# The second bank of a paired product gets a tile of its own: three matrix stages on one Trainium2 core

## The chip, the cores and the metric

The kernel is one program on one core of a Trainium2 chip. TensorE (PE) multiplies, VectorE (DVE), ScalarE (ACT) and GpSimd (POOL) do the elementwise work, SyncE (SP) issues the transfers. The metric is the device time of one execution in microseconds (us), lower is better.

## The reference

Attention over 4 batches, 8 heads, 576 positions and 64 columns a head, half of the heads with a local mask and half with a strided one, followed by two feed-forward layers over the 2304 tokens that it gives:

```
attn = softmax(where(mask, q @ k.T / 8, -1e9));  x = attn @ v          # to 2304 x 512
h = x @ w_in;  x = maximum(0.01 * h, h) @ w_out                        # 512 -> 2048 -> 512
h = x @ w_in2; out = (maximum(h, 0) + log1p(exp(-abs(h)))) @ w_out2    # 512 -> 2048 -> 512
```

## The kernel before

Every product is made of three 16-bit products: each operand is cut into a high and a low part, and high x high, high x low and low x high are added up in PSUM. The tokens go through the layers in units of 288 (first layer) and 256 (second layer). Units 0 to 3 (batches 0 and 1) take the first layer's first product one by one. Units 4 and 5 (batch 2), and units 6 and 7 (batch 3), take it in pairs, by a scheme of seven products of half-size blocks in place of eight (`plan_first_pair`). That scheme, run twice, is what this document is about; "the first pair stage" is units 4 and 5, "the second pair stage" units 6 and 7.

A pair stage has eight blocks, numbered k = 0 to 7 here. One block is seven groups of six matmuls on PE (`group`, L1236, each matmul 128 x 128 by 128 x 288) into three PSUM accumulators, and between them short steps on ACT and DVE that read an accumulator. Their names in the code:

- accumulator a takes p1, then p2 on top of it. Between the two, `t1` (ACT, L1257) copies it to the SBUF tile n1; after p2, `bend11` (ACT, L1272, in the rows `t<-h,gs`) reads it for the last time.
- accumulator b takes p6, p7 and p4 on top of each other. After p6, `u2` (DVE, L1260) adds it to n1 and writes n2; after p7, `u3` (DVE, L1260) does the same for n2's other half; after p4, `c21` (DVE, L1260) reads it for the last time.
- accumulator c takes p5 and then p3, and is read by `c22` and `c12` (DVE, L1260, in the rows `t<-c,t`).
- then come `bend21`, `bend2` (ACT, L1272), the cut into high parts (ACT, L1279) and low parts (POOL, L1283).

So p2 needs t1, u2 needs p6 and t1, p7 needs u2, u3 needs p7, p4 and c22 need u3, p3 needs c22. In the rows of PE, `h<-x,w` is p1 or p2, `h<-sums` is p6 or p7, `h<-sums,w` is p4, `c<-sums` is p5 and `c<-x,w` is p3.

PSUM has four pools: `ps_mm` ("mm", two tiles of two banks), `ps_sc` ("sc", the scores: one tile of two banks), `ps_pt` ("pt", one bank) and `ps_pv` ("po", the value products: one bank). In the kernel before, a and b of a block are the two banks of one "mm" tile, `st["ab"]`; c is the "pt" bank.

The order of everything is written out: `Plan` collects 2018 steps with their needs and the PSUM places that they take and free, and runs them in the order of the table `ORDER`. Each engine takes its instructions in that order. The waits between engines are put in from the tiles that each instruction reads and writes. Beside the pair stages the same table places the last steps of batch 3's attention, the preparation of the second layer's weights (long DVE and ACT steps over 2048 columns, L267, L322, L333, L1497, L1515, L1519) and the products into the first layer's output (`plan_second`, names M and S in the table's steps; `o<-g,pair` in the rows of PE, moved out by ACT, L1330).

Of the kernel before, what the change touches and what calls it, by code (L numbers as in the profile page):

```python
# [11 lines left out]
F32 = mybir.dt.float32  # L12
# [8 lines left out]
P = 128  # L21
# [137 lines left out]
def build(tc, qt, kl, ks, v, wi1, wo1, wi2, wo2, mloc, mstr, msml, out):  # L159
    nc = tc.nc  # L160
    with ExitStack() as ctx:
# [1051 lines left out]
        def plan_first_pair(u, after, places, rank):  # L1213
            b = u // 2
            out, begun = [None] * NF, []
            for k in range(NP):
# [27 lines left out]
                def p1(st=st, q=q, i=i, start=start):  # L1244
                    start()
                    group(st, 0, raw(q, 0, i), xs_of(0, 0), True)
# [643 lines left out]
```

## Time and profile before

| | us |
|---|---|
| median of 3 runs | 833.27 (832.67 to 833.44) |
| the profiled execution | 833.24 |
| its span, first to last instruction | 831.4 |
| PE busy | 806.7 |
| DVE busy | 603.2 |
| ACT busy | 537.3 |

The profiled execution's own time is 1.84 us longer than its span, and 0.03 us from the median. A matmul's busy time here runs until its modelled end, so that the next one starts while it is still "busy"; idle time of PE is time in which no matmul was in flight.

### The profile page before, as it was taken

To read this page: it belongs to the slowest core of one execution; us is meant where nothing else is said; L and a number is where in the kernel's file an instruction comes from. 1 tells how busy PE (TensorE), PEld (TensorE's weight loads), DVE (VectorE), ACT (ScalarE), POOL (GpSimd) and SP (SyncE) were. 2 spreads that over 40 slices of the span, in tenths; PEclk is the share of its full clock that TensorE was granted. 3 is DMA by queue.
4 is the path that set the end of the run, shared out by engine and by line. 5 is a ranking of instruction groups with operands and counts; after the bars stand their busy time and mean duration, and the time that the engine had idled before them with its cause. 6 is when DMAs were issued, how large, how long until landed. Compare 5 with 4: busy or idle time off the path is not lost.

```text
span 831.4 us, 18276 instructions
## 1 busy us (share of the span) xinstructions
PE 806.7 (97%) x7531; PEld 667.6 (80%) x7531; DVE 603.2 (73%) x1367; ACT 537.3 (65%) x957; POOL 253.1 (30%) x193
## 2 busy tenths in 40 slices
PE   9999999999999998998899999999999999999997
PEld 6677777777777766776677888888888888888886
DVE  4999987668899857997678478776656656745654
ACT  2798877764444666355554298776778668766773
POOL 1236946460131243003420024322232222322231
PEclk9999999999999999999999999999999999999999
DMA  9926705342522220631322500100110010000010
GB/s 341 419 103 234 247 16 109 62 135 93 147 62 41 62 102 2 218 130 41 122 81 91 194 4 1 52 1 2 50 53 2 2 52 1 27 1 2 1 52 26
DMA packets 39699, 70.23 MB, mean 84 GB/s; under 512 B 21088, under 2 KB 31168, under 8 KB 37056
## 3 DMA queue, kind: packets, MB, share of 16 engines
q1 hardware_dynamic: 39328, 68.84, 25.1%
q8 instruction: 59, 0.97, 0.5%
q10 hardware_dynamic: 288, 0.23, 0.1%
q14 instruction: 24, 0.20, 0.1%
HBM read 54.84 MB, written 9.44 MB: 77 GB/s over the span
## 4 chain that ended last, share of the span: by engine, by line
PE 82%; DVE 11%; ACT 3%; issue 2%; DMA 2%; DVEq 0%; POOL 0%; ACTq 0%; POOLq 0%
PE o L765 13%; PE o L767 13%; PE o L766 13%; PE h L765 10%; PE h L767 10%; PE h L766 10%; PE h L1236 6%; PE c L1236 2%; PE idle L197 1%; PE ps L490 1%; DVE t L1260 1%; DMA pair<-wi_dram 1%; PE po L700 1%; DVE pair L333 1%; PE ps L495 1%
## 5 line engine op out<-in xcount | busy, mean ns | idle before, releaser
L765 PE MATMUL h<-x,w 128*128 128x256 f16 (+1 forms) x832 | 230.4, 277 | 0.6 <-ACT t L786 0.6
L767 PE MATMUL h<-x,w 128*128 128x256 f16 (+1 forms) x832 | 230.2, 277 | 0.0
L766 PE MATMUL h<-x,w 128*128 128x256 f16 (+1 forms) x832 | 230.2, 277 | 0.0
L1659 POOL TENSOR_TENSOR rs<-rs,t 128x512 f32<-128x512 f32 x72 | 98.2, 1365 | 281.7 <-ACT t L1655 145.9
L765 PE MATMUL o<-g,pair 128*128 128x288 f16 x512 | 146.5, 286 | 0.0
L767 PE MATMUL o<-g,pair 128*128 128x288 f16 x512 | 146.4, 286 | 0.0
L766 PE MATMUL o<-g,pair 128*128 128x288 f16 x512 | 146.4, 286 | 0.0
L1667 DVE TENSOR_TENSOR rs<-rs 128x128 f32<-128x128 f32 x288 | 76.9, 309 | 75.1 <-POOL rs L1659 72.4
L1675 DVE SCALAR_TENSOR_TENSOR gr<-rs,x2g,gr 128x896 f16<-128x896 f32 x72 | 84.9, 1184 | 40.5 <-ACT gr L1671 39.6
L1671 ACT ACTIVATE gr<-rs,x2g 128x896 f16<-128x896 f32 x72 | 74.3, 1036 | 36.6 <-DVE rs L1667 36.6
L765 PEld LDWEIGHTS <-w 128*128 128x128 f16 x832 | 81.4, 98 | 13.9 <-issue 0.2
L766 PEld LDWEIGHTS <-w 128*128 128x128 f16 x832 | 81.4, 98 | 13.0 <-issue 0.7
L767 PEld LDWEIGHTS <-w 128*128 128x128 f16 x832 | 81.4, 98 | 12.9
L614 POOL TENSOR_TENSOR s<-s,sm 128x288 f32<-128x288 f32 (+6 forms) x48 | 43.0, 913 | 147.8 <-DVE sm L609 84.1
L1283 POOL TENSOR_TENSOR g<-t,g 128x576 f16<-128x576 f32 x32 | 45.1, 1415 | 113.0 <-ACT g L1279 111.4
L1642 ACT ACTIVATE t<-h,x2s 128x512 f32<-128x512 f32 x72 | 48.9, 680 | 35.1 <-PE h L767 35.0
L792 POOL TENSOR_TENSOR g<-t,g 128x576 f16<-128x576 f32 x32 | 54.4, 1720 | 22.0 <-ACT g L789 21.8
L765 PEld LDWEIGHTS <-pair 128*128 128x128 f16 x512 | 50.1, 98 | 13.5
L767 PEld LDWEIGHTS <-pair 128*128 128x128 f16 x512 | 50.1, 98 | 12.6
L766 PEld LDWEIGHTS <-pair 128*128 128x128 f16 x512 | 50.1, 98 | 12.3
L765 PE MATMUL o<-w,gr 128*128 128x256 f16 x216 | 58.9, 273 | 0.0
L766 PE MATMUL o<-w,gr 128*128 128x256 f16 x216 | 58.9, 273 | 0.0
(162 smaller groups left out, 1742.6 us busy)
## 6 DMA issues: line engine op xcount, KB each, us to landing
pair<-wi_dram SPq DMA_DIRECT2D x8, 2048.0 KB, 9.7
pair<-wo_dram SPq DMA_DIRECT2D x8, 2048.0 KB, 8.0
x<-t SPq DMA_DIRECT2D x16, 288.0 KB, 2.6
x<-x SPq DMA_DIRECT2D x9, 512.0 KB, 5.1
out_dram<-pair SPq DMA_DIRECT2D x18, 256.0 KB, 2.6
v<-v_dram SPq DMA_DIRECT2D x2, 1856.0 KB, 13.6
pair<-v_dram SPq DMA_DIRECT2D x2, 1408.0 KB, 6.8
q<-qt_dram SPq DMA_DIRECT2D x6, 288.0 KB, 5.9
```

Of the source, the lines that this page charges most:

```text
L614: nc.gpsimd.tensor_tensor(out=sv, in0=sv, in1=rs, op=ALU.mult)
L765: nc.tensor.matmul(ps, ah, bh, start=first, stop=False)
L766: nc.tensor.matmul(ps, ah, bl, start=False, stop=False)
L767: nc.tensor.matmul(ps, al, bh, start=False, stop=last)
L792: nc.gpsimd.tensor_tensor(out=g[:, 1, f : f + 2, :], in0=t, in1=g[:, 0, f : f + 2, :], op=ALU.subtract)
L1236: nc.tensor.matmul(ps, w[:, c], x[:, c], start=first and c == n == 0, stop=c == 1 and n == 2, skip_group_check=not first)
L1283: nc.gpsimd.tensor_tensor(out=g_[:, 1, fs, :], in0=st[f"n{j + 1}"], in1=g_[:, 0, fs, :], op=ALU.subtract)
L1642: nc.scalar.activation(t, self.ps[k], AF.Prelu, scale=self.sc[:, k // 2 : k // 2 + 1], alpha=-1.0)
L1659: nc.gpsimd.tensor_tensor(out=r, in0=r, in1=self.a[k], op=ALU.add)
L1667: nc.vector.tensor_tensor(out=r[:, o], in0=r[:, x], in1=r[:, y], op=op)
L1671: nc.scalar.activation(self.a[k][:, 0], self.r[k][:, 1:], AF.Copy, scale=self.ag[:, k // 2 : k // 2 + 1])
L1675: nc.vector.scalar_tensor_tensor(out=a[:, 1], in0=self.r[k][:, 1:], scalar=self.ag[:, k // 2 : k // 2 + 1], in1=a[:, 0], op0=ALU.mult, op1 ...
```

## The change

Accumulator b leaves the tile that it shared with a. Accumulator a is now the first bank of a two-bank "mm" tile of its own (the second bank of it stays unused), and b is a tile named `b`: the "sc" pool's in blocks 0, 2, 4 and 6, the "po" pool's in blocks 1, 3, 5 and 7. The place of a is given back after `bend11` and no longer after `bend21`; that of b after `c21`. The products of unit 6 into the first layer's output, which took the "sc" tile, now take an "mm" tile as those of the other units do. One condition is changed for the matmuls that fill PE's waits before the first products (`idle`). The table `ORDER` is made anew, all of it.

```diff
 ORDER = (
-    0, 1, 9, 10, 11, 8, 12, 2, 13, 14, 15, 16, 25, 41, 26, 17, 4, 27, 3, 42, 18, 5, 19, 20, 21, 22, 28, 29, 30, 31,
+    0, 9, 10, 11, 12, 1, 13, 25, 26, 8, 114, 14, 2, 41, 27, 3, 15, 19, 16, 17, 28, 4, 42, 43, 18, 29, 20, 21, 5, 30,
...
-                        if n > 0 and y not in o.take and free[y][i] is not None and free[y][i] <= clock[o.eng]:
+                        if n > 0 and y not in o.take and None not in free[y] and free[y][i] <= clock[o.eng]:
...
-                    st["ab"] = two_banks("h")[:, :, :U1]
+                    st["a"] = two_banks("h")[:, 0, :U1]
...
-                    ps = st["c"] if key == "c" else st["ab"][:, key]
+                    if key == "b" and first:
+                        t = ps_pv.tile([P, 512], F32, name="b", tag="po") if st["k"] % 2 else two_banks("b", "sc")[:, 0]
+                        st["b"] = t[:, :U1]
+                    ps = st[key]
...
-                y6 = step("PE", 0.737, p6, [y1], 1)
+                y6 = step("PE", 0.737, p6, [y1], 1, take=["po" if k % 2 else "sc"])
...
-                z21 = step("DVE", 0.4, c21, [y4], 9)
+                z21 = step("DVE", 0.4, c21, [y4], 9, free=[y6])
...
-                e11 = step("ACT", 0.5, bend11, [y2], 5)
-                e21 = step("ACT", 0.5, bend21, [z21, e11], 10, free=[y1])
+                e11 = step("ACT", 0.5, bend11, [y2], 5, free=[y1])
+                e21 = step("ACT", 0.5, bend21, [z21, e11], 10)
...
-                s[u + j] = plan_second(u + j, g[u + j], o1, by("M", k + 16 + 32 * j), s[2][0], "sc" if u + j == 6 else "mm")
+                s[u + j] = plan_second(u + j, g[u + j], o1, by("M", k + 16 + 32 * j), s[2][0])
```

What the change does to the instructions is shown at three places, with the semaphore waits in brackets. The first is PE in the first pair stage, where the first p2 of block 0 follows another group. Before, p1 of block 1 (tile h_3684) ends and p2 of block 0 (tile h_3659) begins:

```order
L1236 MATMUL h_3684<-x_2071,w_673 128x288
L1236 LDWEIGHTS w_674
L1236 MATMUL h_3684<-x_2071,w_674 128x288
L1236 LDWEIGHTS w_673
L1236 MATMUL h_3659<-x_2071,w_673 128x288 [waits DVE_49]
L1236 LDWEIGHTS w_673
```

Now another group stands before it in the new order, and p2 of block 0 (tile h_3665) begins so:

```order
L1239 MATMUL b_3672<-sums_3059,sums_2699 128x288
L1239 LDWEIGHTS sums_2699
L1239 MATMUL b_3672<-sums_3059,sums_2699 128x288
L1239 LDWEIGHTS w_659
L1239 MATMUL h_3665<-x_2043,w_659 128x288 [waits Activation_49]
L1239 LDWEIGHTS w_659
```

The wait of p2 moved from DVE, which reads only accumulator b, to ACT, whose `t1` reads accumulator a; and p7 of block 0 now stands ahead of p2.

The second place is ACT at the start of the second pair stage. L1515 (L1518 after) is a long cut of the second layer's weights. Before:

```order
L1330 ACTIVATE t<-o,xs 128x576 [waits PE_49,Pool_49]
L1257 ACTIVATE t<-h 128x288 [waits PE_49]
L1257 ACTIVATE t<-h 128x288 [waits DMAHW2_49,PE_49,Activation_49]
L1272 ACTIVATE t<-h,gs_476 128x288 [waits DVE_49]
L1515 ACTIVATE pair_128<-pair_127 128x2048 [waits Activation_49]
L1272 ACTIVATE t<-t,gs_476 128x288
L1279 ACTIVATE g<-t 128x2x288 [waits Activation_49]
```

And after the change:

```order
L1333 ACTIVATE t<-o,xs 128x576 [waits PE_49]
L1260 ACTIVATE t<-h 128x288 [waits PE_49]
L1275 ACTIVATE t<-h,gs_503 128x288 [waits PE_49]
L1260 ACTIVATE t<-h 128x288 [waits DMAHW2_49,PE_49,Activation_49]
L1518 ACTIVATE pair_128<-pair_127 128x2048 [waits DVE_49,Activation_49]
L1275 ACTIVATE t<-t,gs_503 128x288 [waits DVE_49]
L1275 ACTIVATE t<-t,gs_503 128x576 [waits DMAHW1_49,DVE_49]
```

`bend11` of block 0 (the row `t<-h,gs`) moved ahead of the second `t1` and waits for PE only, and the long cut behind it waits for DVE's differences alone.

The third place is PE in the products into the output. After the first pair stage the last group is now p2 of block 7 (tile h_4094), where it was p3, and the next product's tile o_4262 waits for ACT:

```order
L1239 LDWEIGHTS w_1370
L1239 MATMUL h_4094<-x_2043,w_1370 128x288
L765 LDWEIGHTS pair0_127
L765 MATMUL o_4262<-g_3664,pair0_127 128x288 [waits Activation_49]
L766 LDWEIGHTS pair0_127
```

Behind the second pair stage, unit 6's second tile o_5638 is opened one small matmul (`pm`) after the last matmul into unit 7's tile o_5501, and waits for ACT too; the two are successive users of one "mm" place, where before they were users of "sc" and "mm":

```order
L767 LDWEIGHTS pair1_128
L767 MATMUL o_5501<-g_4746,pair1_128 128x288
L230 LDWEIGHTS m_5441
L230 MATMUL pm_5636<-idb_113,m_5441 128x128 [waits Activation_49]
L765 LDWEIGHTS pair0_127
L765 MATMUL o_5638<-g_4745,pair0_127 128x288 [waits Activation_49]
```

Both waits stand in front of all that PE has queued behind them.

## Rows read from the trace of the kernel before

**Rows 1.** The page: PE's granted clock in 40 slices of the span (tenths).

```profile
PEclk9999999999999999999999999999999999999999
```

**Rows 2.** Busy time of PE, PEld, DVE, ACT, POOL (instructions) by stage, clock, DMA share, GB/s.

```profile
...
51.00:275.00 224.00, 222.48 (x2159) 175.46 (x2156) 189.31 (x449) 147.55 (x365) 98.47 (x65) 1.00 0.38 107
275.00:324.90 49.90, 44.16 (x363) 33.92 (x362) 32.81 (x77) 30.71 (x60) 20.71 (x16) 1.00 0.20 64
...
372.90:427.10 54.20, 46.01 (x363) 35.22 (x362) 38.58 (x66) 30.90 (x50) 18.22 (x13) 1.00 0.19 65
427.10:800.00 372.90, 372.90 (x3379) 330.00 (x3378) 241.99 (x564) 261.91 (x376) 96.31 (x71) 1.00 0.10 34
```

**Rows 3.** PE's waits in the pair stages: us in total, times, longest.

```profile
PE h L1236 <- DVE t L1260: 7.2, 9, 1.9
PE h L1236 <- ACT t L1272: 3.7, 4, 1.5
PE h L1236 <- ACT t L1257: 2.9, 3, 1.8
```

**Rows 4.** PE, first pair stage, in time: start, us, idle before and releaser.

```profile
276.47 0.90 PE L1236 MATMUL h<-x,w 128*128 128x288 f16 x6
277.63 0.90 PE L1236 MATMUL h<-x,w 128*128 128x288 f16 x6 [0.26 <-DVE t L1260]
278.36 0.90 PE L1236 MATMUL h<-sums 128*128 128x288 f16 x6
...
306.98 0.90 PE L1236 MATMUL h<-sums 128*128 128x288 f16 x6 [0.82 <-ACT t L1272]
...
317.31 0.90 PE L1236 MATMUL h<-sums 128*128 128x288 f16 x6
318.77 0.90 PE L1236 MATMUL h<-x,w 128*128 128x288 f16 x6 [0.56 <-ACT t L1257]
320.31 0.90 PE L1236 MATMUL h<-sums 128*128 128x288 f16 x6 [0.65 <-DVE t L1260]
...
323.48 0.90 PE L1236 MATMUL h<-sums,w 128*128 128x288 f16 x6 [1.54 <-ACT t L1272]
```

**Rows 5.** DVE and ACT at the end of the first pair stage, in time.

```profile
318.30 0.41 ACT L1257 ACTIVATE t<-h 128x288 f32<-128x288 f32 x1 [0.58 <-PE h L1236]
...
319.80 0.46 DVE L1260 SCALAR_TENSOR_TENSOR t<-h,t 128x288 f32<-128x288 f32 x1 [1.17 <-PE h L1236]
...
322.45 0.45 DVE L1260 SCALAR_TENSOR_TENSOR t<-h,t 128x288 f32<-128x288 f32 x1
```

**Rows 6.** PE, second pair stage, in time: four of its eight waits.

```profile
386.01 0.90 PE L1236 MATMUL h<-sums,w 128*128 128x288 f16 x6 [1.90 <-DVE t L1260]
...
405.30 0.90 PE L1236 MATMUL h<-sums 128*128 128x288 f16 x6 [1.81 <-ACT t L1257]
...
415.47 0.90 PE L1236 MATMUL h<-x,w 128*128 128x288 f16 x6 [0.66 <-DVE t L1260]
...
424.93 0.90 PE L1236 MATMUL h<-x,w 128*128 128x288 f16 x6 [1.21 <-DVE t L1260]
```

**Rows 7.** The chain that ended last, 379 to 386 us: start, us, what.

```profile
379.12 0.38 DVE t L1260
...
380.47 0.47 DVE t L1260
...
380.96 0.50 ACT t L1272
381.47 1.81 ACT pair L1515
...
383.30 2.29 DVE pair L1519
```

**Rows 8.** Durations by line: ns min/median/max, first and last start, forms.

```profile
L1260 DVE SCALAR_TENSOR_TENSOR t<-h,t x48: 443/458/459, 277.1 to 426.6; 128x288 f32<-128x288 f32 x48
...
L1330 ACT ACTIVATE t<-o,xs x18: 493/724/742, 191.4 to 471.8; 128x576 f32<-128x576 f32 x14, 128x288 f32<-128x288 f32 x4
```

More of the change, by code (lines that the diff above doesn't have):

```diff
@@ L1217, in plan_first_pair @@
                 q, i = divmod(k, 2)
-                st = {}
+                st = {"k": k}
                 f = 4 * q + i
@@ L1245, in p1 @@
                     start()
-                    group(st, 0, raw(q, 0, i), xs_of(0, 0), True)
-                p2 = lambda st=st, q=q, i=i: group(st, 0, raw(q, 1, i), xs_of(1, 0), False)
-                p6 = lambda st=st, q=q, i=i: group(st, 1, piece(q, 1, i), ts_of(1), True)
-                p7 = lambda st=st, q=q, i=i: group(st, 1, piece(q, 2, i), ts_of(2), False)
-                p4 = lambda st=st, q=q, i=i: group(st, 1, raw(q, 3, i), ts_of(3), False)
+                    group(st, "a", raw(q, 0, i), xs_of(0, 0), True)
+                p2 = lambda st=st, q=q, i=i: group(st, "a", raw(q, 1, i), xs_of(1, 0), False)
+                p6 = lambda st=st, q=q, i=i: group(st, "b", piece(q, 1, i), ts_of(1), True)
+                p7 = lambda st=st, q=q, i=i: group(st, "b", piece(q, 2, i), ts_of(2), False)
+                p4 = lambda st=st, q=q, i=i: group(st, "b", raw(q, 3, i), ts_of(3), False)
                 p5 = lambda st=st, q=q, i=i: group(st, "c", piece(q, 0, i), ts_of(0), True)
@@ L1256, in t1 @@
                     st["n1"] = tmp.tile([P, 2, U1], F32, name="t", tag="t")
-                    nc.scalar.activation(st["n1"][:, 1], st["ab"][:, 0], AF.Copy)
+                    nc.scalar.activation(st["n1"][:, 1], st["a"], AF.Copy)
                 def put(o, ps, y):
@@ L1263, in u2 @@
                     st["n2"] = tmp.tile([P, 2, U1], F32, name="t", tag="t")
-                    put(st["n2"][:, 0], st["ab"][:, 1], st["n1"][:, 1])
-                u3 = lambda st=st: put(st["n2"][:, 1], st["ab"][:, 1], st["n1"][:, 1])
-                c21 = lambda st=st: put(st["n1"][:, 1], st["ab"][:, 1], st["n1"][:, 1])
+                    put(st["n2"][:, 0], st["b"], st["n1"][:, 1])
+                u3 = lambda st=st: put(st["n2"][:, 1], st["b"], st["n1"][:, 1])
+                c21 = lambda st=st: put(st["n1"][:, 1], st["b"], st["n1"][:, 1])
                 c22 = lambda st=st: put(st["n2"][:, 1], st["c"], st["n2"][:, 1])
@@ L1272, in bend @@
                     nc.scalar.activation(o, y, AF.Prelu, scale=gates[q], alpha=0.01)
-                bend11 = lambda st=st, bend=bend: bend(st["n1"][:, 0], st["ab"][:, 0])
+                bend11 = lambda st=st, bend=bend: bend(st["n1"][:, 0], st["a"])
                 bend21 = lambda st=st, bend=bend: bend(st["n1"][:, 1], st["n1"][:, 1])
```

192 rows, old and new, of the table ORDER are left out of this document.

## The prediction

> **What bounds the kernel now.** I read the stages first. From 427.1 to 800 us PE is busy for 372.90 of 372.90 us, and from 51 to 275 us for 222.48 of 224.00; in the two pair stages it is busy for 44.16 of 49.90 and 46.01 of 54.20 us [rows 2]. So PE sets the pace from 51 us on, and the pair stages hold its idle time: 5.7 + 8.2 = 13.9 us. PE's waits give the same sum by releaser: 7.2 us in nine waits for L1260 on DVE, 3.7 in four for L1272 and 2.9 in three for L1257 on ACT, 13.8 us in 16 waits [rows 3].
>
> What a wait costs is a little more than its idle time, because a matmul's modelled end hides its last part. From 276.47 to 277.63 is 1.16 us, from 277.63 to the next group 0.73, which is what a group costs where nothing waits: 0.43 us lost where the row says 0.26 [rows 4]. At 0.17 more for each of 16 waits the two stages lose 13.8 + 2.7 = 16.5 us. With all of it gone the kernel would take 833.24 - 16.5 = 816.7 us; that is the most that the change can give there.
>
> Then I asked of each wait whether the arithmetic needs it. At 277.63 a p2 waits for DVE, whose steps read only accumulator b, while p2 writes a. At 306.98 a p6, which writes b afresh, waits for L1272 on ACT, whose steps read only a [rows 4]. At 318.77 p2 waits for t1, which is needed; but t1 starts at 318.30, 0.09 after the end of p6 (317.31 + 0.90 = 318.21), the group that stands between p1 and p2 and that t1 doesn't read [rows 4, 5]. At 320.31 p7 waits for u2, which starts at 319.80, 0.13 after the end of that p2, which it doesn't read either. So reads and writes of a and b are kept in the order of the program as if the two banks were one: they are one tile. The trace shows no price for this but the waits themselves.
>
> Sorted in this way, eleven of the 16 are coupled: all seven for ACT (3.7 + 2.9), three p2 that wait for DVE (0.26, 0.66 and the 1.21 at 424.93) and the p7 at 320.31 (0.65) [rows 3, 4, 6]: 9.4 us of idle time, 11.3 with 0.17 each. Two of them hide a needed wait. The p4 at 323.48 needs u3, which ends at 322.45 + 0.45 = 322.90 [rows 5], so 0.5 of its 1.7 us is coupling. The p2 at 424.93 can move ahead by one group, but the p4 behind it needs the same DVE step, so 0.7 of 1.4 is won. That leaves 11.3 - 1.2 - 0.7 = **9.4 us coupled**, and 16.5 - 9.4 = **7.1 us needed**.
>
> **The change, part by part.**
>
> *Accumulator b in a tile of its own.* p2 then waits for ACT's t1 alone, as the new order's first place shows, and p4, p6 and p7 for DVE or for nobody. The 9.4 us go, if nothing else stands behind them. What can: the block's own chain. From p7 to p4 it takes 0.90 (group) + 0.13 + 0.46 (u3) + 0.05 = 1.54 us with the hops of rows 4 and 5, so p7 itself and one more group behind it (1.47) hide all but 0.07. In the new order at least one more stands between them in all 16 blocks. Where DVE or ACT is in a long step of weight work when its turn comes, a wait is left. Bounds: 0, and half of 9.4, since a coupled wait and the next needed one lie on the same chain. I take 1.5 us, nearer to the lower end, because a is freed by bend11 and lets p1 of the block after next go early.
>
> The Trainium skill, page "PSUM — Partial Sum Buffer", in its summary of rules for kernel authors, tells to guard PSUM by bank, and to let engines read one bank while the matmul fills another. By that rule none of the eleven waits was needed, and their sum would be the full 9.4 us; by the rows of before a program that guards the whole tile pays for them, and by the bounds above 4.7 to 9.4 come back.
>
> *The needed waits.* They are behind long DVE steps. The largest is the p4 at 386.01, 1.90 + 0.17 us. Its chain: a DVE step that ends at 380.94 releases a bend11 (380.96), the long cut L1515 queues behind that (381.47, 1.81 us), then L1519 on DVE (2.29), then u3, then p4 [rows 6, 7]. In the new order bend11 stands earlier and waits for PE alone, and the long cut needs only DVE's differences, which ended before 379.12. It can start 2.3 us earlier, and the wait of 2.07 is covered but for DVE steps of 0.46 that stand in front; I leave 0.5. Of the other 5.0 us I can show no such move, since long DVE steps stand among the same steps as before, with one group more or less between; I take 3.0 as left. So 3.5 of 7.1 stay (bounds 0 and 7.1).
>
> *Two new waits.* Both come from places in "mm". After the first pair stage p2 of block 7 is the last group, and the next product takes the place that its bend11 frees: 0.90 + 0.13 + 0.50 (L1272 [rows 7]) + 0.05 = 1.58, less the 0.73 that the group takes anyway: 0.85 us. Behind the second pair stage unit 6's second tile needs the place that unit 7's tile leaves after its move to SBUF: the matmul's 0.29 + 0.13 + 0.74 (L1330 [rows 8]) + 0.05 = 1.21, less 0.18 for two matmuls' issue: 1.0 us. Before, unit 6 had "sc" to itself there. Together 1.9 us, in the open, with all of PE's queue behind them.
>
> *The order elsewhere.* From 427 us on there is no idle time to win, and from 51 to 275 us 1.5 us at most. In the first 51 us DVE and ACT prepare and PE's gaps are partly filled with idle matmuls; the steps that lead to the first product stand in nearly the same order. I take 0 for all of it, and 1 us either way inside the range.
>
> The sum: -9.4 + 1.5 - (7.1 - 3.5) + 1.9 = -9.6, and 833.24 - 9.6 = **823.6 us**. The profiled execution is 0.03 us below the median, so this is the median's forecast too. The best corner is -9.4 - 7.1 + 1.9 = -14.6 (818.6 us), the worst -9.4 + 4.7 + 1.9 = -2.8 (830.4 us).
>
> **The rivals.**
>
> *The waits move.* b of the odd blocks shares its one bank with batch 3's last value products, two of which stand inside the first pair stage in the new order, and DVE must read the bank empty each time. If a long DVE step such as L1519's 2.29 us stands in front of that read both times, 4.6 us come back, and the kernel takes about 828; with the worst corner, 830.4. For it: DVE is busy for 66 and 71% of the two stages [rows 2]. Against it: where DVE is free the read costs PE 0.07 us by the count above. Chance 0.16 for 828 to 831.5.
>
> *The banks don't matter* (it ends on the other side). If DVE and ACT, each in its own order, set the pace of a block, then p2 and p6 run earlier only to wait one step later, the 16.5 us stay, and the two new waits are added: 833.24 + 1.9 = 835.1 us. It decides where less than about 0.2 us of 16.5 comes back. For it: five of the 16 waits are of this kind. Against it: in eleven the step waited for reads another bank, or waited itself for a group that it doesn't read. Chance 0.05. A recovery of about 2 us, eaten by the new waits, would look like no change: 0.06.
>
> *The clock.* PE's granted clock is 1.00 through both stages in spite of 16 waits of up to 1.9 us [rows 2, 3], and nine tenths or more in every slice [rows 1]; a pair stage at half of it would take its 56 groups of 0.73 us once more, 41 us, and the kernel 865. The Trainium skill, "TensorE: Matmul & The Clock Gate", section on psum-queue depth-cycling, warns that short idle times between groups that cycle through PSUM banks can bring the clock down, and the change cycles through more of them; the trace of before doesn't bear it out. Chance 0.01.
>
> **How the numbers follow.** The forecast's case, 819 to 828, has 0.70; 828 to 831.5 has 0.16; within 0.2% of before (1.7 us, about what a measurement of this kernel can tell from no change) 0.06; slower 0.06; below 819, 0.02. Faster is 0.88. The range from 819 to 830 leaves out the last three and a part of the second case, about 2 in 10.
>
> **What would show it.** Right: PE's waits on the accumulators fall from 13.8 to about 6 us of idle time, none of them a p2 behind DVE or a p4, p6 or p7 behind L1257's and L1272's successors, save where the value products share the bank; two new waits of 0.7 to 1.0 us at the first matmuls of `o<-g,pair`, on ACT; the stages from 275 to 427 us shorter by some 11 us, and the products between and after them longer by 1 or 2; the rest unchanged. Wrong: waits for L1260's successor that grow by as much as the others shrink; a wait for the "po" bank by a value product or by an odd block; a first product later than at 51 us; or idle time after 427 us, if the second layer's weights are no longer ready when PE comes 10 us earlier.

## The result, and the profile after

| | before | after |
|---|---|---|
| median, us | 833.09 (832.67 to 833.44, 4 runs) | 820.01 (819.95 to 821.11, 4 runs) |
| the profiled execution, and its span | 833.24, 831.4 | 819.95, 818.2 |
| first group of the first pair stage to the second layer's first matmul | 196.52 | 182.15 |
| from there to PE's last matmul | 353.93 | 356.15 |
| from there to the end | 5.96 | 4.98 |

The ratio is 0.9846, with a 95% interval from 0.9829 to 0.9863. The three stretches are differences of starts in the timeline: 274.99, 471.51 and 825.44 us before, 274.92, 457.07 and 813.22 after. In each of them PE does the same matmuls in both kernels, but for one small matmul of 0.06 us that the new order puts behind the second layer's first matmul (`pm` in the rows: it spreads the largest entry of a set of weights to all partitions). So they show where the 13.2 us of span are: 14.4 won up to the second layer, and 1.2 lost behind it.

The page of the changed kernel, answering to [rows 1]:

```profile
span 818.2 us, 18283 instructions
...
PEclk9999999999999999999999999999999999999999
```

Busy time by stage of the changed kernel, answering to [rows 2] (PE, PEld, DVE, ACT, POOL, then clock, DMA share, GB/s):

```profile
51.00:274.90 223.90, 222.49 (x2159) 175.86 (x2157) 186.66 (x459) 147.64 (x365) 94.98 (x65) 1.00 0.40 121
274.90:320.50 45.60, 44.69 (x375) 35.10 (x373) 31.43 (x70) 29.81 (x60) 20.14 (x16) 1.00 0.21 68
...
366.50:411.70 45.20, 44.60 (x363) 35.24 (x362) 36.97 (x65) 30.73 (x49) 19.12 (x13) 1.00 0.22 77
...
457.00:813.20 356.20, 354.36 (x3248) 317.30 (x3247) 230.04 (x536) 262.20 (x381) 97.76 (x72) 1.00 0.07 23
```

PE's idle time in the two pair stages is 0.9 + 0.6 us, where it was 5.7 + 8.2, though twelve products `o<-g,pair` (1.47 us) now stand inside the first of them. New is 1.8 us of idle time behind 457 us. PE's waits by releaser, answering to [rows 3] (us in total, times, longest; L1239 is the groups' line, L1263 the additions on DVE, L1275 bend11, L1333 the move of an output tile):

```profile
PE o L765 <- DVE pair L1710: 1.1, 1, 1.1
PE o L765 <- ACT t L1333: 0.8, 1, 0.8
PE o L767 <- DVE gr L1678: 0.8, 1, 0.8
...
PE b L1239 <- DVE t L1263: 0.6, 2, 0.4
PE o L765 <- ACT t L1275: 0.6, 1, 0.6
PE c L1239 <- DVE t L1263: 0.4, 1, 0.4
```

Three waits on the accumulators are left, where there were 16, and all three are for DVE: two p4 and a p3. None is for ACT, and no p2 waits for DVE. The same in time, with the two waits that were forecast (PE; start, us, idle before and releaser), answering to [rows 4, 6]:

```profile
285.21 0.90 PE L1239 MATMUL b<-sums,w 128*128 128x288 f16 x6
286.50 0.90 PE L1239 MATMUL c<-x,w 128*128 128x288 f16 x6 [0.39 <-DVE t L1263]
...
319.09 0.90 PE L1239 MATMUL h<-x,w 128*128 128x288 f16 x6
320.58 0.28 PE L765 MATMUL o<-g,pair 128*128 128x288 f16 x1 [0.59 <-ACT t L1275]
...
376.17 0.90 PE L1239 MATMUL h<-x,w 128*128 128x288 f16 x6
377.25 0.90 PE L1239 MATMUL b<-sums,w 128*128 128x288 f16 x6 [0.17 <-DVE t L1263]
...
381.65 0.90 PE L1239 MATMUL b<-sums 128*128 128x288 f16 x6
382.98 0.90 PE L1239 MATMUL b<-sums,w 128*128 128x288 f16 x6 [0.43 <-DVE t L1263]
...
444.21 0.22 PE L230 MATMUL pm<-idb,m 128*128 128x128 bf16 x1
445.26 0.28 PE L765 MATMUL o<-g,pair 128*128 128x288 f16 x1 [0.83 <-ACT t L1333]
```

From start to start, less the 0.73 or 0.74 us of a group, the three lose 0.56, 0.34 and 0.60 us: 1.5 us, where the 16 of before lost 16.5. The two new waits cost 1.49 - 0.73 = 0.76 and 1.05 - 0.06 = 0.99 us; 0.06 is what a `pm` takes from its start to the next where nothing waits (444.51 to 444.57 in run 6 below).

### The profile page after: what moved, and what is told of

It is laid out like the page before. It is cut to its first block, busy times and chain, and to the rows that moved or that the text cites. A ratio compares the mean times of both kernels' runs of the same rounds, so it can differ in the third digit from the quotient of the medians.

```text
span 818.2 us, 18283 instructions
## 1 busy us (share of the span) xinstructions
PE 804.2 (98%) x7534; PEld 668.5 (82%) x7534; DVE 598.4 (73%) x1367; ACT 536.5 (66%) x957; POOL 250.4 (31%) x193
## 4 chain that ended last, share of the span: by engine, by line
PE 85%; DVE 7%; ACT 4%; DMA 1%; issue 1%; POOL 1%; DVEq 0%; ACTq 0%; POOLq 0%
PE o L765 13%; PE o L767 13%; PE o L766 13%; PE h L765 10%; PE h L767 10%; PE h L766 10%; PE b L1239 4%; PE c L1239 2%; PE h L1239 2%; PE ps L495 1%; PE po L700 1%; DVE rs L1670 1%; PE ps L490 1%; DMA pair<-wi_dram 1%; PE po L695 1%
## 5 line engine op out<-in xcount | busy, mean ns | idle before, releaser
L1670 DVE TENSOR_TENSOR rs<-rs 128x128 f32<-128x128 f32 x288 | 78.7, 315 | 72.9 <-POOL rs L1662 70.4
L1678 DVE SCALAR_TENSOR_TENSOR gr<-rs,x2g,gr 128x896 f16<-128x896 f32 x72 | 86.5, 1206 | 40.0 <-ACT gr L1674 38.9
L765 PEld LDWEIGHTS <-w 128*128 128x128 f16 x832 | 81.4, 98 | 13.8 <-issue 0.2
L1286 POOL TENSOR_TENSOR g<-t,g 128x576 f16<-128x576 f32 x32 | 45.4, 1432 | 94.2 <-ACT g L1282 92.2
L765 PE MATMUL o<-w,gr 128*128 128x256 f16 x216 | 58.9, 273 | 1.1 <-DVE pair L1710 1.1
L767 PE MATMUL o<-w,gr 128*128 128x256 f16 x216 | 58.9, 273 | 0.0
L766 PE MATMUL o<-w,gr 128*128 128x256 f16 x216 | 58.9, 273 | 0.0
```

The lines of the kernel that those rows point to most:

```text
L765: nc.tensor.matmul(ps, ah, bh, start=first, stop=False)
L766: nc.tensor.matmul(ps, ah, bl, start=False, stop=False)
L767: nc.tensor.matmul(ps, al, bh, start=False, stop=last)
L1286: nc.gpsimd.tensor_tensor(out=g_[:, 1, fs, :], in0=st[f"n{j + 1}"], in1=g_[:, 0, fs, :], op=ALU.subtract)
L1670: nc.vector.tensor_tensor(out=r[:, o], in0=r[:, x], in1=r[:, y], op=op)
L1678: nc.vector.scalar_tensor_tensor(out=a[:, 1], in0=self.r[k][:, 1:], scalar=self.ag[:, k // 2 : k // 2 + 1], in1=a[:, 0], op0=ALU.mult, op1 ...
```

## The experiments

Every run below was timed beside the kernel before. The stretches are those of the table above: from the first group of the first pair stage to the second layer's first matmul, from there to PE's last matmul, from there to the end. They come from one profiled execution of each kernel.

| run | median, us | ratio, 95% interval | stretches, us |
|---|---|---|---|
| before (its medians beside the others) | 832.83 to 833.55 | | 196.52, 353.93, 5.96 |
| the change | 820.01 | 0.9829 to 0.9863 | 182.15, 356.15, 4.98 |
| 1 order of before, own tile | 824.13 | 0.9877 to 0.9904 | 186.86, 354.03, 6.07 |
| 2 new order, one tile | 837.04 | 1.0034 to 1.0060 | 198.90, 356.18, 4.94 |
| 3 order of before, own tile, one place | 830.62 | 0.9959 to 0.9982 | 194.54, 354.04, 6.00 |
| 4 before, bend11 moved | 830.70 | 0.9964 to 0.9982 | 194.66, 353.92, 6.01 |
| 5 two waits less | 819.35 | 0.9818 to 0.9845 | 181.43, 356.19, 4.94 |
| 6 of these, the place alone | 819.84 | 0.9828 to 0.9861 | 181.37, 356.19, 4.92 |
| 7 of these, the group alone | 820.13 | 0.9828 to 0.9855 | 182.38, 356.20, 4.93 |
| 8 run 5, small matmul later | 818.61 | 0.9818 to 0.9844 | 181.36, 356.19, 4.90 |
| 9 run 8, last reads behind | 818.87 | 0.9816 to 0.9843 | 181.48, 354.96, 5.93 |
| 10 run 8, tail of before from the second layer's first product | 822.59 | 0.9865 to 0.9892 | 181.06, 360.04, 5.98 |
| 11 run 8, tail of before from some 80 steps later | 819.16 | 0.9822 to 0.9848 | 181.26, 354.43, 5.93 |

The first group of the pair stages began between 274.1 and 276.1 us in these profiles, also in kernels with the same program up to there. A difference under 1 us between two of the last seven runs is therefore read from the stretches, not from the medians. The stretches have a spread too: runs 8 to 11 have the same program up to the second layer's first product, and their first stretch is 181.06 to 181.48 us, so less than about 0.4 us says nothing there. Behind it, kernels with the same order agree within 0.12 us.

Where an order is joined to tiles that it wasn't made for, a step whose PSUM place isn't free, or that needs such a step, runs at the first moment at which it can:

```diff
+                for i in order:
+                    late.append(self.ops[i])
+                    while o := next((o for o in late if can(o)), None):
+                        late.remove(o)
+                        yield o
```

**The tile and the order apart (runs 1 and 2).** My theory was that the un-coupling gains; the rival, that the new order does. Run 1 is the changed kernel with the table of before, and with unit 6 in the scores' tile:

```diff
 ORDER = (
-    0, 9, 10, 11, 12, 1, 13, 25, 26, 8, 114, 14, 2, 41, 27, 3, 15, 19, 16, 17, 28, 4, 42, 43, 18, 29, 20, 21, 5, 30,
+    0, 1, 9, 10, 11, 8, 12, 2, 13, 14, 15, 16, 25, 41, 26, 17, 4, 27, 3, 42, 18, 5, 19, 20, 21, 22, 28, 29, 30, 31,
...
-                s[u + j] = plan_second(u + j, g[u + j], o1, by("M", k + 16 + 32 * j), s[2][0])
+                s[u + j] = plan_second(u + j, g[u + j], o1, by("M", k + 16 + 32 * j), s[2][0], "sc" if u + j == 6 else "mm")
```

> The tiles of the change with the order of before: accumulator b is a tile of its own (the scores' place in even blocks, the value products' place in odd ones), a has an 'mm' tile, unit 6 keeps the scores' tile, and the table ORDER is that of the kernel before. Five steps whose place isn't free yet run some steps later. If the un-coupling of the two banks is what gains (my theory), the waits on PE for ACT in the pair stages and most of those of a p2 for DVE go without any new order: 833.1 - 9.4 gives 823.7 us, with the allowance of 1.5 us 825.2; the wait of 2.07 us in front of the second pair stage's first p4 stays, since the long cut stands where it stood. If the new order is what gains, and the tile only lets it be written, this run stays at 831 to 834 us.

Run 2 is the other half: the tiles and places of before under the new table.

```diff
 ORDER = (
-    0, 1, 9, 10, 11, 8, 12, 2, 13, 14, 15, 16, 25, 41, 26, 17, 4, 27, 3, 42, 18, 5, 19, 20, 21, 22, 28, 29, 30, 31,
+    0, 9, 10, 11, 12, 1, 13, 25, 26, 8, 114, 14, 2, 41, 27, 3, 15, 19, 16, 17, 28, 4, 42, 43, 18, 29, 20, 21, 5, 30,
...
-                        if n > 0 and y not in o.take and free[y][i] is not None and free[y][i] <= clock[o.eng]:
+                        if n > 0 and y not in o.take and None not in free[y] and free[y][i] <= clock[o.eng]:
```

> The order of the change with the tiles of before: a and b are again the two banks of one 'mm' tile, which is given back after bend21, and unit 6's products are in the scores' place. Seven steps whose place isn't free yet run some steps later (six of them a p1, which must wait for the longer-held tile). My theory: the reads and writes of a and b are kept in program order again, so the new order has at least as much of coupled waits as the old one: PE's waits on the accumulators 10 us or more, and 830 to 838 us. If the new order is what gains, 820 to 824 us.

Run 1 took 824.13 us, 8.8 less than before; run 2 took 837.04, 4.1 more. PE's waits of run 1, then of run 2 (L1259 and L1256 are the groups' lines, L1283 and L1280 DVE's additions, L757 the value products' last read, L1295 and L1292 the line of bend11, L1277 t1). The last row of run 1 is a p6 of block 3, at 296.77: its place is the value products' bank, and it needs the DVE step L757, which reads that bank and ended at 296.62, and no step of L1295.

```profile
PE c L1259 <- DVE t L1283: 2.3, 1, 2.3
...
PE b L1259 <- DVE t L1283: 1.5, 5, 0.4
...
PE b L1259 <- DVE x L757: 0.8, 1, 0.8
...
PE b L1259 <- ACT t L1295: 0.4, 1, 0.4
```

```profile
PE h L1256 <- DVE t L1280: 12.1, 11, 2.6
PE h L1256 <- ACT t L1292: 1.8, 2, 1.4
...
PE h L1256 <- ACT t L1277: 1.1, 2, 0.6
```

So the tile gains without any new order, and the new order without the tile loses: PE's waits for DVE grow from 7.2 us [rows 3] to 12.1. With the own tile the same order wins another 186.86 - 182.15 = 4.7 us up to the second layer, and gives 1.0 us back behind it; run 2 gives back 1.2 there against before. Two things stay open. What an order made anew for the shared tile would reach no run shows. And run 1 joins three things, b's own tile, its second place, and a's place given back earlier: run 3 takes the second away, the third was not tried by itself.

Run 1 shows one thing more. The p4 that waited 1.90 us at 386.01 [rows 6] waits 0.17 us, though its place in the order is that of before. It is the p4 of block 1, and the chain in front of it begins with bend11 of block 0. That chain in run 1 (ACT: bend11 L1295 and the long cut L1538; DVE: u2 of block 0, then its c21 as the second of the two at 377.08; PE: the p4):

```profile
373.56 0.50 ACT L1295 ACTIVATE t<-h,gs 128x288 f32<-128x288 f32 x1 [0.28 <-PE h L1259]
376.39 1.91 ACT L1538 ACTIVATE pair<-pair 128x2048 f16<-128x2048 f32 x1 [2.33 <-DVE pair L1520]
...
373.32 0.45 DVE L1283 SCALAR_TENSOR_TENSOR t<-b,t 128x288 f32<-128x288 f32 x1
...
377.08 1.03 DVE L1283 SCALAR_TENSOR_TENSOR t<-b,t 128x288 f32<-128x288 f32 x2
...
381.47 0.90 PE L1259 MATMUL b<-sums,w 128*128 128x288 f16 x6 [0.17 <-DVE t L1283]
```

bend11 reads a while DVE reads b, and starts when p2 has ended. Before, it came behind c21 in the order, and ran at 380.96, behind the DVE step that ended at 380.94 [rows 7]. Both only read PSUM, so two readers of one tile were kept in order too, and what I had called a needed wait was a coupled one. (bend11 also writes one half of the SBUF tile n1, whose other half u2 reads and c21 writes. n1 is one tile in run 1 as well, and bend11 runs beside u2 there, so it isn't n1 that keeps them in order.)

Two more of the five waits that I had called needed are coupled: the p7 of block 4 in either stage, 0.65 us at 301.59 and 0.48 us at 399.65, waits no more in run 1. The first of the two in the kernel before (PE: p2 and p7; DVE: u2):

```profile
300.05 0.90 PE L1236 MATMUL h<-x,w 128*128 128x288 f16 x6
301.59 0.90 PE L1236 MATMUL h<-sums 128*128 128x288 f16 x6 [0.65 <-DVE t L1260]
...
301.08 0.46 DVE L1260 SCALAR_TENSOR_TENSOR t<-h,t 128x288 f32<-128x288 f32 x1 [1.11 <-PE h L1236]
```

u2 starts 0.13 us after the end of that p2 (300.05 + 0.90 = 300.95), which it doesn't read: the sign that the prediction had found at 320.31. In the second pair stage of run 1 four waits are left of eight, that of 381.47 above and these, all p4:

```profile
376.72 0.90 PE L1259 MATMUL b<-sums,w 128*128 128x288 f16 x6 [0.26 <-DVE t L1283]
...
387.20 0.90 PE L1259 MATMUL b<-sums,w 128*128 128x288 f16 x6 [0.43 <-DVE t L1283]
...
415.26 0.90 PE L1259 MATMUL b<-sums,w 128*128 128x288 f16 x6 [0.41 <-DVE t L1283]
```

**Is that so, in the kernel before itself? (run 4)** One step moves; op 983 is bend11 of block 0, 976 its p7, 975 its u2:

```diff
-    975, 1219, 976, 977, 963, 978, 993, 991, 994, 995, 979, 981, 980, 982, 983, 1220,
+    975, 1219, 983, 976, 977, 963, 978, 993, 991, 994, 995, 979, 981, 980, 982, 1220,
```

> The kernel before, with its tile and its order but for one step: bend11 of block 0 of the second pair stage stands right behind u2 in the order, ahead of p7, instead of behind c21. In the trace of before it was released by DVE (380.96), and the long cut L1515 behind it at 381.36, and the first p4 then waited 1.90 us at 386.01. My theory, formed from the run with the old order and the own tile, where this bend11 was released by PE: its wait for DVE was coupled too (c21 reads b, bend11 reads a of the same tile), not one of the arithmetic. Then bend11 goes at about 378, the long cut starts when DVE's differences are done, 2.2 us earlier, the wait of 1.90 us falls under 0.4, and the kernel takes 831.4 us. Rival: the long DVE steps set the pace there, the wait moves on to the next p4 or p2, and the kernel stays within 0.5 us of 832.9.

It took 830.70 us, 2.1 less, where 1.5 were expected. The long cut before, then bend11 (L1243), the long cut (L1486) and the p4 (L1207) of run 4:

```profile
381.36 1.90 ACT L1515 ACTIVATE pair<-pair 128x2048 f16<-128x2048 f32 x1
```

```profile
376.43 0.50 ACT L1243 ACTIVATE t<-h,gs 128x288 f32<-128x288 f32 x1 [1.61 <-DVE t L1231]
...
379.01 1.91 ACT L1486 ACTIVATE pair<-pair 128x2048 f16<-128x2048 f32 x1 [1.79 <-DVE pair L1468]
...
384.09 0.90 PE L1207 MATMUL h<-sums,w 128*128 128x288 f16 x6 [0.18 <-DVE t L1231]
```

The long cut starts 2.35 us earlier (381.36 to 379.01; 0.18 of it is the earlier start of the first pair stage), and the wait of 1.90 us is 0.18, as expected. And bend11 itself, in one tile, still waits 1.61 us for u2's read of b, which stands ahead of it, where in run 1 it ran beside it. The Trainium skill, "PSUM — Partial Sum Buffer", section "Terms", says that two engines on one bank at once are a collision, reads against reads included. That is a rule for one bank, which no run here puts to the test; a and b are two, and run 1 shows reads of both at once.

**The turns (run 3).** Run 1 with b in the scores' tile in all blocks:

```diff
-                        t = ps_pv.tile([P, 512], F32, name="b", tag="po") if st["k"] % 2 else two_banks("b", "sc")[:, 0]
+                        t = two_banks("b", "sc")[:, 0]
...
-                y6 = step("PE", 0.737, p6, [y1], 1, take=["po" if k % 2 else "sc"])
+                y6 = step("PE", 0.737, p6, [y1], 1, take=["sc"])
```

> As the first run (order of before, b a tile of its own), but b in the scores' place in all blocks. Sixteen steps run later than in that order, most of them a p6 that must wait until the block before has given its b back. If a tile of its own is what counts and not the turns, this run is within 2 us of the first one: 824 to 827 us. If the turns count, each p6 waits for the c21 of the block before: where p6 stands right behind p4 this costs 0.90 + 0.13 + 0.46 + 0.05 - 0.73 = 0.8 us, in up to 14 blocks 11 us, so 829 to 836 us. I lean to some of both: 828.

It took 830.62 us, 6.5 more than run 1 and 2.6 more than I leant to. The waits of its groups for DVE's additions are one row:

```profile
PE b L1259 <- DVE t L1283: 11.3, 14, 1.6
```

So a tile of its own with one place keeps 2.3 of the 8.8 us. The waits for ACT are gone, and b's groups wait for DVE in their place. Seven of the 14 are a p6 that needs the read by c21 of the block before: 4.0 us in all, 0.55 us of idle time in five of them, which with 0.17 is 0.7 where 0.8 was expected. The other 7.3 us are six p4 and a p7; that they wait because each p6 in front of them comes later is likely, and not shown. In this order the turns are worth more than the un-coupling alone.

**The two new waits (runs 5 to 8).** Run 5 takes both away (op 908 is p2 of block 7, 917 its bend11):

```diff
-    906, 912, 913, 914, 903, 908, 1186, 917, 915,
+    906, 908, 917, 912, 913, 914, 903, 1186, 915,
...
-            over = plan.add("PE", 0.1, U.over, [y], rank("X", 0), take=["mm" if u else "po"])
+            over = plan.add("PE", 0.1, U.over, [y], rank("X", 0), take=["mm" if u > 1 else "po"])
```

> The changed kernel with its two new waits taken away: p2 of block 7 in the first pair stage, with its bend11, stands ahead of p4 and p3 instead of behind them, so that the place of a is free when the next products want it; and the small matmul that opens unit 1 of the second layer takes the value products' bank in place of an 'mm' place, so that unit 6's second tile gets the other 'mm' place. My theory (both waits lie in the open on PE): 0.75 - 0.12 and 1.05 - 0.24 us come back, 1.4 us, 818.6 us. If PE's queue behind them has its own next wait (an operand of the second layer's weights, or the end on DVE), less than 0.5 us comes back: 819.5 to 820.

Both waits went, but the stretch fell by 0.72 us and not by 1.4. A small matmul (`pm`) now waits for the largest entry of a quarter of weights. In the changed kernel (DVE, then the `pm` and the matmul before it):

```profile
334.62 2.29 DVE L267 TENSOR_REDUCE m<-pair 128x1 f32<-128x2048 f32 x1 [1.08 <-DMA pair<-wi_dram]
...
336.62 0.29 PE L767 MATMUL o<-g,pair 128*128 128x288 f16 x1
336.96 0.23 PE L230 MATMUL pm<-idb,m 128*128 128x128 bf16 x1
```

and in run 5:

```profile
335.20 2.29 DVE L238 TENSOR_REDUCE m<-pair 128x1 f32<-128x2048 f32 x1 [1.34 <-DMA pair<-wi_dram]
...
337.54 0.23 PE L201 MATMUL pm<-idb,m 128*128 128x128 bf16 x1 [1.06 <-DVE m L238]
```

The entry was ready at 334.62 + 2.29 = 336.91, 0.05 us ahead of its reader. So PE waited there in the changed kernel too: from 336.62 to 336.96 are 0.34 us, where one such product takes 0.12. No row shows it, since the modelled end of the matmul before it, 336.91, hides it. Whatever PE wins ahead of such a place is lost there. Runs 6 and 7 do one part each:

> Of the run with two waits less only the second part: the small matmul that opens unit 1 of the second layer takes the value products' bank, p2 of block 7 stands where the change put it. By the trace of that run this is the part that gained: from the first group of the first pair stage to the second layer's first product 182.15 - 0.93 = 181.2 us, and 819.1 us as the median, if the start is that of the changed kernel. If the two parts need each other, 181.8 or more.

> Of the run with two waits less only the first part: p2 of block 7 and its bend11 ahead of p4 and p3. The wait of 0.6 us behind the first pair stage goes, but PE then comes 0.76 us earlier to the small matmul that needs the largest entry of the third quarter, which in the changed kernel started 0.05 us after that entry was ready (336.91 and 336.96): the gain is eaten there, the same stretch takes 182.1 to 182.4 us, and the kernel 820 us. If the 1.06 us wait there came from something else in that run, this run shows 181.4 us and 819.2.

The place alone gives 181.37 us, all of the gain; the group alone 182.38, none, with 1.0 us of wait at the same `pm`. Run 8 moves that `pm` behind the next twelve matmuls, 1.47 us of products (op 1193; 1194 and 1196 are the DVE steps that need it, 948 the products):

```diff
-    1193, 1195, 1194, 1196, 1201, 967, 948,
+    1195, 948, 1193, 1194, 1196, 1201, 967,
```

> The kernel of the run with two waits less, and one more move: the small matmul that spreads the largest entry of the third quarter of the second layer's first weights, with its two DVE steps, stands 24 matmuls (1.47 us of products) later. In the run before it waited 1.06 us for the DVE maximum L238, which itself waited for the transfer of the weights; so the gain of the first wait removed was eaten there. If that account is right, the wait goes without a new one, the stretch from the first to the second pair stage is 1.0 to 1.1 us shorter (46.98 before), and the kernel takes 818.3 us. If DVE's chain behind the maximum (the scaling and the cuts that the second pair stage needs) is what is late, the same time is lost at a later small matmul or at the second pair stage's first groups, and it stays at 819.3.

The stretch is 181.36 us, the same as run 5's: the expectation's rival held. From the first product behind the first pair stage to the second pair stage it is 0.80 us shorter (46.98 to 46.18), and from there to that stage's last group 0.72 longer (44.49 to 45.21), since the first p4 of that stage now waits, which in run 5 it didn't:

```profile
371.92 0.90 PE L1210 MATMUL b<-sums,w 128*128 128x288 f16 x6 [0.53 <-DVE t L1234]
```

The median of 818.61 us is the lowest here, but a good part of it is a start that was 1.1 us earlier than run 5's in the profile; its interval overlaps that of the change.

**The tail (runs 9 to 11).** Behind the second layer's first matmul the new order costs 361.13 - 359.89 = 1.24 us. Its wait for L1710 stands 1.5 us ahead of PE's last matmul, and what it waits for, in the changed kernel:

```profile
810.65 0.47 ACT L1707 ACTIVATE pair<-o,x2b 128x256 f32<-128x256 f32 x1 [5.27 <-PE o L767]
811.16 0.48 DVE L1710 SCALAR_TENSOR_TENSOR pair<-o,x2b,pair 128x256 f32<-128x256 f32 x1 [4.47 <-ACT pair L1707]
...
811.70 0.27 PE L765 MATMUL o<-w,gr 128*128 128x256 f16 x1 [1.08 <-DVE pair L1710]
```

ACT's L1707 and DVE's L1710 both read the first bank of the scores' two-bank tile, and the products that wait write the second. Run 9 puts the two reads (ops 2010, 2011) behind PE's last products, as before had them:

```diff
-    2006, 2010, 2011, 1927, 2007, 2008, 2009, 2012,
+    2006, 1927, 2007, 2008, 2009, 2010, 2011, 2012,
```

> The kernel of the small matmul that stands later, and in the last unit of the second layer the first two reads of the accumulators (ACT's move and DVE's first combination, both of the first bank of the scores' tile) stand behind all of PE's last products in the order, as in the kernel before. My theory: the wait of 1.08 us of PE for L1710 at the end of the changed kernel is the same coupling, of two banks of one tile (the products behind it write the second bank of that tile); it goes, PE's last matmul comes 1.2 us earlier, but the reads come later against it, so that the end behind PE's last matmul grows from 4.9 to 5.9 us, and the time stays within 0.5 us of 818.6. If the wait is one for the operand (the cut of the last sums), PE waits there as before, and the reads behind it make the kernel 1 us slower.

The wait is gone, the stretch 1.23 us shorter, the end 1.03 longer: it was the same coupling, and the early reads nearly paid for it, within 0.2 us. Runs 10 and 11 take the table of before for the tail, from the second layer's first product on, and from some 80 steps later:

> As the run beside it, and from the first product of the second layer on, the order of before. In the changed kernel the stretch from that product's first matmul to PE's last one took 356.15 us, where before it took 353.93; two waits in it, 0.8 us for the cut L1678 and 1.08 us for L1710, are not in the trace of before; and the end behind PE's last matmul is 4.98 us, where it was 5.96. If the order of the tail alone makes this difference, 1.2 us come back: 817.1 us. If the tail is late because the second layer's weights and inputs come later against PE, which is 14 us earlier there, the waits stay or others take their place: 818.3 us or more.

> The kernel of the small matmul that stands later, with the order of before from the place on where unit 2's scale has been spread (some 80 steps behind the second layer's first product); the earlier try at this took the order of before from that first product on, and PE then waited 3.1 us for unit 2's largest entry, a step that the order of before has in front of that place. If the new order of the tail is what costs, the waits for L1678 (0.8 us) and L1710 (1.08 us) go, the stretch from the first product of the second layer to PE's last matmul falls from 356.2 to 354 us, the end behind it grows by 1 us, and the kernel takes 817.4 us. If PE's coming 15 us earlier is what costs there, the waits stay or move, and it takes 818.6 or more.

Run 10 says nothing on the tail: a small matmul for unit 2 stood too early, and PE waited 3.1 us. In run 11 both waits are gone, and stretch and end together take 360.36 us, where run 8 takes 361.09 and before 359.89. So 0.7 of the 1.2 us comes back with the order. The other 0.5 is in the trace: 0.06 is the `pm` that stands in this stretch now, and 0.40, from start to start, is a wait for ACT, 55.1 us behind the second layer's first matmul, where the change waits for L1678 at 55.9:

```profile
512.48 0.27 PE L736 MATMUL h<-x,w 128*128 128x256 f16 x1 [0.23 <-ACT rs L1641]
```

Why DVE and ACT are late there, against before, no run shows. The median, 819.16 against 818.61 us for run 8, doesn't show the gain.

## Why the prediction was right, and what was mis-sized

823.6 us were forecast, 820.0 measured, near the lower end of the range: the mechanism and its places held, and the sum was short by 3.6 us. By the steps of the sum, against the span's -13.2:

- *Coupled waits, -9.4.* That they go with the tile, without a new order, is shown by run 1. Their size was taken too small. In run 1's second stage, where no other wait comes in, 8.1 us of idle time in eight waits become 1.3 in four. Over both stages 12.5 of the 13.8 us are gone, and 3.9 us of other waits come in, all in the first stage. The first stretch is 9.7 us shorter by the difference of the two, so that it comes so near to 9.4 is luck.
- *What stands behind them, +1.5.* In the order of before it is those 3.9 us of idle time, most of it a p5 that waits 2.3 us for c and two p6 that wait 0.8 and 0.4 for the value products' reads. In the new order 0.56 us is left, at a p3 (286.50).
- *Needed waits, 7.1 to 3.5.* This is the step that was mis-sized: 0.34 and 0.60 us are left of them, at two p4. The sorting was wrong. The 2.07 us at 386.01 were coupled as well, through two readers of one tile (runs 1 and 4); I had the chain right and its first link wrong, and so left 0.5. The two p7 of block 4 were coupled too (run 1), the first by the very sign that I had found at 320.31 and hadn't looked for there. Of the 5.0 us beside the 2.07 I kept 3.0, for want of a move that I could show in the new order. Together with the allowance I kept 5.0 us of waits on the accumulators; 1.5 are left.
- *Two new waits, +1.9.* 0.76 and 0.99 us at the two places, for 0.85 and 1.0. Run 6 shows what the second is worth. By run 7 the first costs nothing by itself, since the weights' largest entry is no earlier without it.
- *The order elsewhere, 0.* Right only as a sum. Up to the second layer 1.12 us more are gone than the pair stages' waits explain: 16.12 against 15.0. About half of it is a `pm` that waited for the same kind of entry: 0.60 us of idle time at 343.35 before, 0.76 from start to start, and 0.22 at 336.96 in the change. Behind the second layer's first matmul 1.24 us are lost. There I had looked only for idle time to win, not for waits that a new order makes, and had named idle time behind 427 us only as a sign that weights weren't ready; what PE waits for there are steps on DVE.

-15.0 + 1.75 - 1.12 + 1.24 - 0.07 (an earlier start) = -13.2.

Of the rivals, "the waits move" is true of run 1 (3.9 us) and of run 3 (11.3), not of the change: two of the value products still stand inside its first pair stage, and none of its waits is for their bank. "The banks don't matter" falls with run 1. The clock was 1.00 in both stages, with groups that go through more banks than before. The warning of the Trainium skill, "TensorE: Matmul & The Clock Gate", section on psum-queue depth-cycling, is not borne out by this trace, which has only three such idle times left; with the 16 of before the clock was 1.00 as well [rows 2].

## What to carry to other kernels

Where waits are put in from tiles, as here, two accumulators with different readers do better in different tiles, even where a bank stays unused; here the one that is refilled soonest wanted a second place as well. Look for waits between engines that touch different halves of one tile, reads behind reads included, and look for the same sign at every wait before you call one needed. Make the order anew after that: this order lost 4.1 us with the tiles that it wasn't made for. And before a wait is taken away, look for the next one behind it. A matmul that starts 0.05 us after its operand is ready is waiting, though no row shows idle time; the distance from the start before it does.

## What had not been expected of the hardware

In the profiled execution of run 10 the granted clock fell while PE waited for the entry of its small matmul, and the second layer's products behind it ran at the lower level (1.2 GHz is 0.5) for some us. PE was idle from 458.46 to 461.55 us. By single us the clock was 1.00 up to 460, 0.75 from 460 to 461, 0.50 from there to 467, 0.84 from 467 to 468, and 1.00 again after it. PE, then busy time by 5 us (the clock is the number behind the five engines):

```profile
461.55 0.29 PE L201 MATMUL pm<-idb,m 128*128 128x128 bf16 x1 [3.09 <-DVE m L1585]
```

```profile
455.00:460.00 5.00, 3.46 (x31) 2.78 (x29) 4.79 (x17) 2.19 (x4) 0.00 (x0) 1.00 0.45 132
460.00:465.00 5.00, 3.45 (x17) 2.50 (x18) 3.14 (x10) 0.96 (x2) 1.26 (x1) 0.55 0.43 138
465.00:470.00 5.00, 5.00 (x38) 4.02 (x36) 0.00 (x0) 2.98 (x5) 0.49 (x1) 0.77 0.00 0
470.00:475.00 5.00, 5.00 (x48) 4.49 (x46) 3.39 (x6) 4.94 (x7) 2.06 (x2) 1.00 0.01 3
```

The wait cost more than itself. The stretch of run 10 is 5.6 us longer than that of run 11, which has a wait of 0.4 us that run 10 hasn't, so 6.0 us are to be explained. The wait is 3.25 of them from start to start. The rest, 2.8 us, is of the size that the clock gives away: PE worked at 0.50 from 461.55 to about 467.3 us, and half of these 5.8 us is 2.9.

It isn't so in every execution. The mean granted clock of run 10's four executions is 0.994 (the profiled one), 0.996, 1.000 and 1.000, and their spans are 821.7, 820.6, 820.0 and 819.4 us: in two of them it can't have fallen in this way. In run 1 a wait of 2.31 us, at 291.85, left the clock at 1.00 from 290 to 295 us, and so did one of 2.57 us in run 2, at 409.42, from 407 to 411. What decides whether it falls these runs don't settle.
